# Transposes moved from TensorE to the DMA crossbar, with a reordered first stage, in an attention and feed-forward kernel

## The chip, the cores and the metric

The kernel runs on one core of one Trainium2 chip. The metric is device time in microseconds (us): the median of several executions. The span of a profile is a little shorter than the time of its execution (456.9 us of 459.06 us before). TensorE is called PE in the profile, its weight loads PEld, VectorE DVE, ScalarE ACT, GpSimd POOL, SyncE SP; POOLq and SPq are the queues on which the last two issue transfers.

## The reference

```python
# q, k, v: 8 batches x 8 heads x 576 positions x 64; 8 global positions
scores = q @ k.T / sqrt(64)
mask = (abs(pos_i - pos_j) <= 32) | is_global[i] | is_global[j]
attn = softmax(where(mask, scores, -1e9))
x = (attn @ v), heads side by side: 4608 tokens x 512
out = x + sigmoid(x @ w_res) * ((gelu(x @ w_gate) * (x @ w_val)) @ w_out)   # d_ff = 1536
```

Inputs and output are f32; the kernel multiplies in bf16.

## The kernel before

A first stage prepares batch 0 and does the attention of the first 512 tokens. Then nine chunks of 512 tokens follow. Twelve steps of the feed-forward input (`ffn_in`) run while the next batch is prepared; sixteen slots of the feed-forward output follow, interleaved with the attention of the next chunk. Instructions keep the order in which the program emits them on each engine. These are the parts that the argument touches (cuts are marked with `# ...`):

```python
def zero_qk(i):                       # fills: unused half of qz, edge columns of kt
    for u in range(2):
        zero_wide(qz[i], 64 - 64 * u, 64, u * S, [[2 * S, NP], [1, S]])
    zero_wide(kt[i], 0, 128, 0, [[S + 64, NP], [1, 32]])           # columns 0..31
    zero_wide(kt[i], 0, 128, 32 + S, [[S + 64, NP], [1, 32]])      # columns 608..639

def zero_rest(i):
    nc.vector.memset(ve[i][:, :, :, D:VG], 1.0)                    # the ones column of ve
    # ... edge partitions of ve, parts of gt and ptg

def prep_pair(b, p, what):            # queries or keys of two heads, batches 1 to 7
    src = q_st if what == "q" else k_st
    ps = pss.tile([128, S], BF16, name=f"t{what}", tag="sc")
    for r in range(NQT):              # 5 tiles of positions
        n = min(128, S - 128 * r)
        nc.tensor.transpose(ps[:, 128 * r:128 * r + n], src[0:n, r, 128 * p:128 * p + 128], ident[0:n, 0:n])
    if what == "q":
        nc.scalar.copy(qt[b % 2][:, p, :], ps)
    else:
        nc.vector.tensor_copy(kt[b % 2][:, p, 32:32 + S], ps)

def turn_x(c, t):                     # attention output of 128 tokens -> xt, the input of ffn_in
    # ... PSUM tile tx
    for kk in range(NKT):             # 4
        nc.tensor.transpose(tx[:, kk, :], xtok[c % 2][:, t, 128 * kk:128 * kk + 128], ident)
    (nc.scalar.copy if c == 0 else nc.vector.tensor_copy)(xt[c % 2][:, :, 128 * t:128 * t + 128], tx)

# end of the first stage: loads that cast to bf16, all on GpSimd's queue
load_qk(1)
load_gate_cols(1024, 1536)            # last third of w_gate and w_val
load_v(1)
# ... w_res, w_out in two halves, gathers of the global rows

for c in range(NCH):
    b = c + 1
    # ... load_v(b) for b > 1
    for j in range(NFF):              # 12 steps
        ffn_in(c, j)
        if c == 0:                    # fills of the second set of buffers
            if j == 0: zero_qk(1)
            elif j == 1: zero_rest(1); hot_rows(1)
            # ...
            if j >= 4: prep_pair(b, (j - 4) // 2, "qk"[j % 2])
        elif j < 8: prep_pair(b, j // 2, "qk"[j % 2])
        # ... c == 1 and j == 8: spread_qk, global rows of the later batches
        if j == (11 if c == 0 else 8):
            shift_v(b); load_qk(b + 1); prep_qz(b, 0, NP)
    # ... slots: scores at 0..7, then for t in 0..3
    #     slots[5 + 2 * t].append(values(c + 1, t))
    #     slots[7 + 2 * t].insert(0, turn_x(c + 1, t))
    # ... each slot runs its list and then a quarter of ffn_out; ffn_out ends with
    #     GpSimd's add into ob and nc.sync.dma_start(out[...], ob)
```

`qt`, `qz`, `kt`, `ve`, `vo`, `gt` and `ptg` exist twice, for even and odd batches.

The softmax here doesn't subtract the row's maximum and nothing guards it: scores larger than these inputs give would overflow.

Of the kernel before, what the change touches and what calls it, by code (L numbers as in the profile page):

```python
# [23 lines left out]
def kernel(  # L24
# [23 lines left out]
    CH = 8  # L48
# [67 lines left out]
    nc.scalar.dma_start(gpi, bass.AP(tensor=g32.tensor, offset=g32.offset, ap=[[0, 16], [2, NG], [1, 1]]))  # L116
    for p in range(NP):
        for src, what in ((q, "q"), (k, "k")):
# [9 lines left out]
    nc.gpsimd.memset(ident, 0.0)  # L128
    nc.gpsimd.affine_select(out=ident, in_=ident, pattern=[[-1, 128]], channel_multiplier=1, base=0,
                            compare_op=ALU.not_equal, fill=1.0)  # L130

    blk = const.tile([128, 16], BF16, name="blk", tag="blk")
    nc.gpsimd.memset(blk, 1.0)
    nc.gpsimd.affine_select(out=blk, in_=blk, pattern=[[-8, 16]], channel_multiplier=1, base=0,
                            compare_op=ALU.is_ge, fill=0.0)
    nc.gpsimd.affine_select(out=blk, in_=blk, pattern=[[8, 16]], channel_multiplier=-1, base=7,
                            compare_op=ALU.is_ge, fill=0.0)
# [20 lines left out]
    def zero_rest(i):  # L158
        nc.vector.memset(ve[i][:, :, :, D:VG], 1.0)
        zero(ve[i][0:32, 0, :, :])  # L160
        zero(ve[i][96:128, 4, :, :])
        zero_wide(gt[i], 0, 128, 0, [[1, 64]])
        zero_wide(gt[i], 0, 128, 64 + S, [[1, 64]])
        zero_wide(ptg[i], 0, 128, 64 * (i % 2), [[128, 5], [1, 64]])
# [4 lines left out]

    sel = const.tile([128, 128], BF16, name="sel", tag="sel")  # L170
# [6 lines left out]
    hrow = const.tile([128, 1], I32, name="hrow", tag="hrow")  # L177
    nc.vector.tensor_single_scalar(hrow, ip, 3, ALU.logical_shift_right)
# [11 lines left out]
    gather("q", 0)  # L190
    load_v(0)
    gather("v", 0)
    load_gate_cols(0, 512)
    load_gate_cols(512, 1024)
# [8 lines left out]
    for n in range(1, B // 2):  # L203
        nc.vector.tensor_single_scalar(idx[:, n:n + 1], idx[:, 0:1], float(2 * H * S * n), ALU.add)
    far = const.tile([128, S], F32, name="far", tag="far")
    nc.scalar.activation(far, iota_f, ACTF.Square, bias=ngp, scale=1.0)
    band = const.tile([128, 64], BF16, name="band", tag="band")
# [5 lines left out]
    nc.gpsimd.memset(band, 1.0)  # L213
    nc.gpsimd.affine_select(out=band, in_=band, pattern=[[-1, 64]], channel_multiplier=1, base=0,
                            compare_op=ALU.is_ge, fill=0.0)
    nc.gpsimd.affine_select(out=band, in_=band, pattern=[[1, 64]], channel_multiplier=-1, base=64,
                            compare_op=ALU.is_ge, fill=0.0)

    def masks():
# [9 lines left out]
        nc.vector.scalar_tensor_tensor(maskg, far, 1024.5, nong, ALU.is_gt, ALU.mult)  # L229

    def hot_rows(i):
        r0 = 64 - 64 * (i % 2)
        nc.vector.tensor_copy(gt[i][r0:r0 + 64, 64:64 + S], hot[r0:r0 + 64, :])
# [6 lines left out]
    def spread_qk(n0, n1):  # L240
        nn = n1 - n0
        for what, big, pstep in (("k", kgz, 144), ("q", qgz, 16)):
# [6 lines left out]
            for e in range(2):  # L249
                shift = 64 * e if what == "k" else 0  # L250
                for u in range(2):
                    nc.vector.tensor_copy(
                        view(big, 64 * u, 64, (2 * n0 + e) * width + shift + 8 * u,
                             [[2 * width, nn], [pstep, NP], [1, NG]]),
                        view(tg, 64 * u, 64, 64 * e + 8 * u, [[128, nn], [16, NP], [1, NG]]))
# [41 lines left out]
    def prep_pair(b, p, what):  # L297
        src = q_st if what == "q" else k_st
        ps = pss.tile([128, S], BF16, name=f"t{what}", tag="sc")
        for r in range(NQT):  # L300
            n = min(128, S - 128 * r)
            nc.tensor.transpose(ps[:, 128 * r:128 * r + n], src[0:n, r, 128 * p:128 * p + 128], ident[0:n, 0:n])  # L302
        if what == "q":
            nc.scalar.copy(qt[b % 2][:, p, :], ps)  # L304
        else:
            nc.vector.tensor_copy(kt[b % 2][:, p, 32:32 + S], ps)
# [264 lines left out]
```

## Time and profile before

| | before |
|---|---|
| time, median of 3 | 461.24 us (460.74 to 461.93) |
| span of the profile; TensorE busy | 456.9 us; 91% |
| global scores of batch 0 start | 32.30 us |
| first feed-forward matmul (first `g_ps`) | 46.3 us |
| `g_ps` of chunk 1, of chunk 2 | 94.65, 144.62 us |
| chunks 2 to 6, mean | 46.47 us each |

A chunk is measured here from its first `g_ps` to that of the next.

```profile
DMA  9999999999999999999999999991010000999999
```

### The profile page before, as it was taken

The numbers are of one execution on the slowest core, as the hardware profiler recorded it, in microseconds if no ns is written. First come the engines' busy times: TensorE is split into PE (matmuls) and PEld (weight loads), VectorE is DVE, ScalarE is ACT, GpSimd is POOL, SyncE is SP. The second block draws the span as 40 slices with busy tenths as digits, with TensorE's granted clock in tenths as the row PEclk, the third lists the DMA queues.
The fourth block names the chain that finished last, engine by engine and source line by source line (L and its number), as shares of the span: only waits on it lengthen the run. The fifth ranks groups of instructions, "written<-read, shape, count | busy, mean of one in ns | idle before, by whom it ended". The sixth has DMA issues, their size and how long they took to land.

```text
span 456.9 us, 7784 instructions
## 1 busy us (share of the span) xinstructions
PE 415.2 (91%) x3119; PEld 232.2 (51%) x3170; DVE 234.7 (51%) x465; ACT 182.6 (40%) x291; POOL 166.6 (36%) x187
## 2 busy tenths in 40 slices
PE   2038899999799999999999999999999999999995
PEld 2027445644465556545654465546554664465442
DVE  6277655634774456435554555355535554364421
ACT  4105445243343345334524462436243623543321
POOL 6965618150594271327133712471240121022013
PEclk9999999999999999999999999999999999999999
DMA  7999939283093990199119921994190010001001
GB/s 192 157 193 185 197 80 96 57 91 54 2 99 97 100 103 24 47 123 101 29 47 122 90 39 47 121 79 50 47 103 20 24 44 28 0 25 70 0 23 70
DMA packets 117092, 35.18 MB, mean 77 GB/s; under 512 B 104576, under 2 KB 111232, under 8 KB 117056
## 3 DMA queue, kind: packets, MB, share of 16 engines
q0 software_dynamic: 108784, 18.62, 54.4%
q1 hardware_dynamic: 8128, 16.06, 11.3%
q8 instruction: 25, 0.41, 0.4%
q14 instruction: 11, 0.09, 0.1%
q10 hardware_dynamic: 144, 0.00, 0.0%
HBM read 39.19 MB, written 9.44 MB: 106 GB/s over the span
## 4 chain that ended last, share of the span: by engine, by line
PE 87%; DVE 5%; POOL 3%; issue 2%; DMA 1%; ACT 1%; POOLq 0%; DVEq 0%
PE g_ps L405 22%; PE v_ps L409 20%; PE f_ps L432 20%; PE r_ps L422 7%; PE nd L377 3%; PE sc L351 3%; PE tk L302 2%; PE tq L302 2%; PE nd L371 2%; PE sn L339 2%; PE sg L317 2%; PE tx L397 2%; DVE qz L310 1%; DMA gpi<-in_global_idx_dram 1%; POOL ve L98 1%
## 5 line engine op out<-in xcount | busy, mean ns | idle before, releaser
L413 DVE SCALAR_TENSOR_TENSOR ht<-gsb,v_ps 128x512 bf16<-128x512 bf16 x108 | 73.9, 687 | 111.8 <-PE v_ps L409 85.1
L438 POOL TENSOR_TENSOR ob<-prb,xtok 128x512 f32<-128x512 f32 x36 | 41.8, 1160 | 203.6 <-DVE prb L436 203.5
L412 ACT ACTIVATE gsb<-g_ps 128x512 bf16<-128x512 f32 x108 | 64.5, 597 | 120.6 <-PE g_ps L405 111.5
L405 PE MATMUL g_ps<-xt,wg_t 128*128 128x512 bf16 x431 | 111.4, 380 | 1.4 <-ACT xt L398 0.7
L409 PE MATMUL v_ps<-xt,wv_t 128*128 128x512 bf16 x415 | 108.8, 379 | 0.5
L432 PE MATMUL f_ps<-wo_t,ht 128*128 128x512 bf16 x408 | 101.8, 379 | 1.3
L409 PEld LDWEIGHTS <-wv_t 128*128 128x128 bf16 x432 | 42.3, 98 | 51.0 <-issue 0.2
L405 PEld LDWEIGHTS <-wg_t 128*128 128x128 bf16 x432 | 37.8, 98 | 41.1 <-issue 1.4
L432 PEld LDWEIGHTS <-ht 128*128 128x128 bf16 x432 | 38.5, 98 | 34.0
L354 ACT ACTIVATE pt<-sc 128x512 bf16<-128x512 f32 x72 | 41.9, 597 | 30.6 <-PE sc L351 30.5
L425 ACT ACTIVATE rsb<-r_ps 128x512 bf16<-128x512 f32 x36 | 21.5, 596 | 65.6 <-PE r_ps L422 51.4
L90 POOL DMA_DIRECT2D q_st<-in_q_dram x35 | 30.4, 890 | 41.6 <-PE tq L302 41.4
L356 DVE TENSOR_TENSOR pt<-pt,maskw 128x512 bf16<-128x512 bf16 x72 | 31.0, 435 | 25.8 <-ACT pt L354 24.5
L436 DVE SCALAR_TENSOR_TENSOR prb<-rsb,f_ps 128x512 f32<-128x512 bf16 x36 | 24.6, 684 | 29.4 <-PE f_ps L432 29.2
L422 PE MATMUL r_ps<-wr_t,xt 128*128 128x512 bf16 x135 | 36.3, 379 | 0.4
L98 POOL DMA_DIRECT2D ve<-in_v_dram x40 | 33.9, 867 | 1.8 <-DMA k_st<-in_k_dram 1.8
L90 POOL DMA_DIRECT2D k_st<-in_k_dram x35 | 31.1, 910 | 4.6 <-DMA wg_t<-in_moe_w_gate_dram 1.6
L351 PE MATMUL sc<-qz,kt 128*128 128x128 bf16 x288 | 27.9, 224 | 1.0 <-DVE qz L310 0.9
L351 PEld LDWEIGHTS <-kt 128*128 128x128 bf16 x288 | 21.4, 100 | 11.2 <-issue 1.0
L304 ACT COPY qt<-tq 128x576 bf16<-128x576 bf16 x28 | 17.9, 638 | 16.8 <-PE tq L302 16.8
L391 DVE TENSOR_TENSOR xtok<-nd,rden 128x512 bf16<-128x512 f32 x34 | 23.5, 691 | 1.2
L377 PEld LDWEIGHTS <-pt 128*128 128x128 bf16 x576 | 22.3, 97 | 1.0
(103 smaller groups left out, 371.2 us busy)
## 6 DMA issues: line engine op xcount, KB each, us to landing
out_dram<-ob SPq DMA_DIRECT2D x36, 256.0 KB, 2.0
vo<-ve SPq DMA_DIRECT2D x16, 260.0 KB, 3.7
q_st<-in_q_dram POOLq DMA_DIRECT2D x28, 128.0 KB, 4.2
k_st<-in_k_dram POOLq DMA_DIRECT2D x28, 128.0 KB, 4.7
ve<-in_v_dram POOLq DMA_DIRECT2D x24, 128.0 KB, 4.4
ve<-in_v_dram POOLq DMA_DIRECT2D x16, 96.0 KB, 7.9
wg_t<-in_moe_w_gate_dram POOLq DMA_DIRECT2D x3, 512.0 KB, 6.4
wv_t<-in_moe_w_val_dram POOLq DMA_DIRECT2D x3, 512.0 KB
```

The source lines that it names most:

```text
L90: nc.gpsimd.dma_start(dst[0:n, r, :].rearrange("p (h d) -> p h d", d=D), src[b].rearrange("h s d -> s h d")[128 * r:128 * r + n])
L98: nc.gpsimd.dma_start(t[p0:p1, c, :, 0:D], v[b].rearrange("h s d -> s h d")[s0 + p0:s0 + p1])
L351: nc.tensor.matmul(sc[:, n, :, :], kt[b % 2][:, p, 64 * i:64 * i + 128], qz[b % 2][:, p, :, 64 * i:64 * i + 64], start=True, stop=True)
L354: nc.scalar.activation(mine, sc, ACTF.Exp, bias=0.0, scale=SCALE)
L377: nc.tensor.matmul(nds[h // 4][:, VG * (h % 4):VG * (h % 4) + VG], view(pt, 0, 128, c0, [[1, 128]]), vw, start=False, stop=(h % 4 == 3 and ...
L405: nc.tensor.matmul(g_ps, wg_t[:, kk, 128 * j:128 * j + 128], x[:, kk, :], start=(kk == 0), stop=(kk == NKT - 1))
L409: nc.tensor.matmul(v_ps, wv_t[:, kk, 128 * j:128 * j + 128], x[:, kk, :], start=(kk == 0), stop=(kk == NKT - 1))
L412: nc.scalar.activation(gsb, g_ps, ACTF.Gelu, bias=0.0, scale=1.0)
L413: nc.vector.scalar_tensor_tensor(ht[:, j, :], gsb, 0.5, v_ps, ALU.mult, ALU.mult)
L422: nc.tensor.matmul(r_ps, xt[c % 2][:, kk, 128 * t:128 * t + 128], wr_t[:, kk, :], start=(kk == 0), stop=(kk == NKT - 1))
L432: nc.tensor.matmul(held["f"], ht[:, j, 128 * t:128 * t + 128], wo_t[:, j, :], start=(j == 0), stop=(j == NFF - 1))
L438: nc.gpsimd.tensor_tensor(ob, prb, xtok[c % 2][:, t, :], ALU.add)
```

## The change

The intent is to take transposes off the bounding engine: the queries and keys of batches 1 to 7, and the inputs of chunks 1 to 8, are transposed by the DMA crossbar, from SyncE's queue. The first stage's fills and masks are spread over the engines so that TensorE starts sooner.

```diff
-    def prep_pair(b, p, what):
-        # ... five TensorE transposes and a copy
+    def turn_qk(b):
+        for src, dst, c0 in ((q_st, qt[b % 2], 0), (k_st, kt[b % 2], 32)):
+            for r in range(NQT):
+                n = min(128, S - 128 * r)
+                nc.sync.dma_start(dst[:, :, c0 + 128 * r:c0 + 128 * r + n], src[0:n, r, :], transpose=True)
...
     def turn_x(c, t):
+        mine = xt[c % 2][:, :, 128 * t:128 * t + 128]
+        if c:
+            nc.sync.dma_start(mine, xtok[c % 2][:, t, :], transpose=True)
+            return
...
     for c in range(NCH):
         b = c + 1
         if b < B:
+            turn_qk(b)
             if b > 1:
                 load_v(b)
...
                     elif j == 1:
-                        zero_rest(1)
+                        zero_rest(1, nc.vector)
-                    if j >= 4:
-                        prep_pair(b, (j - 4) // 2, "qk"[j % 2])
-                elif j < 8:
-                    prep_pair(b, j // 2, "qk"[j % 2])
+                if c == 1:
+                    if j == 6:            # was 8
+                        spread_qk(1, B // 2)
...
-                if j == (11 if c == 0 else 8):
+                if j == 8:
                     shift_v(b)
# first stage, in words: the band mask made ahead of GpSimd's transfer issues; fill of pt to ScalarE;
# zero_rest(0) to GpSimd; load of the global positions on SyncE; masks before the first transposes;
# hot_rows and the qgz copies to ScalarE; w_gate and w_val columns 512:1024 loaded later
```

More of the change, by code (lines that the diff above doesn't have):

```diff
@@ L115 @@
     g32 = global_idx.bitcast(I32)
-    nc.scalar.dma_start(gpi, bass.AP(tensor=g32.tensor, offset=g32.offset, ap=[[0, 16], [2, NG], [1, 1]]))
+    nc.sync.dma_start(gpi, bass.AP(tensor=g32.tensor, offset=g32.offset, ap=[[0, 16], [2, NG], [1, 1]]))
     for p in range(NP):
@@ L127 @@
     ident = const.tile([128, 128], BF16, name="ident", tag="ident")
+    band = const.tile([128, 64], BF16, name="band", tag="band")
+    blk = const.tile([128, 16], BF16, name="blk", tag="blk")
     nc.gpsimd.memset(ident, 0.0)
-    nc.gpsimd.affine_select(out=ident, in_=ident, pattern=[[-1, 128]], channel_multiplier=1, base=0,
-                            compare_op=ALU.not_equal, fill=1.0)
-    blk = const.tile([128, 16], BF16, name="blk", tag="blk")
+    nc.gpsimd.memset(band, 1.0)
     nc.gpsimd.memset(blk, 1.0)
-    nc.gpsimd.affine_select(out=blk, in_=blk, pattern=[[-8, 16]], channel_multiplier=1, base=0,
-                            compare_op=ALU.is_ge, fill=0.0)
-    nc.gpsimd.affine_select(out=blk, in_=blk, pattern=[[8, 16]], channel_multiplier=-1, base=7,
-                            compare_op=ALU.is_ge, fill=0.0)
+    for t, pattern, mult, base, op, fill in (
+            (ident, [[-1, 128]], 1, 0, ALU.not_equal, 1.0),
+            (band, [[-1, 64]], 1, 0, ALU.is_ge, 0.0), (band, [[1, 64]], -1, 64, ALU.is_ge, 0.0),
+            (blk, [[-8, 16]], 1, 0, ALU.is_ge, 0.0), (blk, [[8, 16]], -1, 7, ALU.is_ge, 0.0)):
+        nc.gpsimd.affine_select(out=t, in_=t, pattern=pattern, channel_multiplier=mult, base=base,
+                                compare_op=op, fill=fill)
     def zero(ap):
@@ L156, in zero_qk, with zero_rest @@
         zero_wide(kt[i], 0, 128, 32 + S, [[S + 64, NP], [1, 32]])
-    def zero_rest(i):
-        nc.vector.memset(ve[i][:, :, :, D:VG], 1.0)
-        zero(ve[i][0:32, 0, :, :])
-        zero(ve[i][96:128, 4, :, :])
-        zero_wide(gt[i], 0, 128, 0, [[1, 64]])
-        zero_wide(gt[i], 0, 128, 64 + S, [[1, 64]])
-        zero_wide(ptg[i], 0, 128, 64 * (i % 2), [[128, 5], [1, 64]])
+    def zero_rest(i, eng):
+        eng.memset(ve[i][:, :, :, D:VG], 1.0)
+        eng.memset(ve[i][0:32, 0, :, :], 0.0)
+        eng.memset(ve[i][96:128, 4, :, :], 0.0)
+        eng.memset(gt[i][:, 0:64], 0.0)
+        eng.memset(gt[i][:, 64 + S:128 + S], 0.0)
+        eng.memset(ptg[i][:, :, 64 * (i % 2):64 * (i % 2) + 64], 0.0)
     def zero_globals(b0, b1):
@@ L168, in zero_globals @@
         zero_wide(qgz, 0, 128, b0 * NP * 16, [[1, (b1 - b0) * NP * 16]])
+    hrow = const.tile([128, 1], I32, name="hrow", tag="hrow")
+    nc.vector.tensor_single_scalar(hrow, ip, 3, ALU.logical_shift_right)
+    none = const.tile([128, 1], F32, name="none", tag="none")
+    zero(none)
+    nc.scalar.copy(view(pt.bitcast(F32), 0, 128, 32, [[64, H * CH], [1, 32]]),
+                   view(none, 0, 128, 0, [[0, H * CH], [0, 32]]))
     sel = const.tile([128, 128], BF16, name="sel", tag="sel")
@@ L174 @@
     zero_globals(0, 2)
-    hrow = const.tile([128, 1], I32, name="hrow", tag="hrow")
-    nc.vector.tensor_single_scalar(hrow, ip, 3, ALU.logical_shift_right)
     idx = const.tile([128, B // 2], I32, name="idx", tag="idx")
@@ L190 @@
     gather("q", 0)
+    zero_rest(0, nc.gpsimd)
     load_v(0)
@@ L193 @@
     load_gate_cols(0, 512)
-    load_gate_cols(512, 1024)
     gpc = const.tile([128, 1], F32, name="gpc", tag="gpc")
@@ L205 @@
     far = const.tile([128, S], F32, name="far", tag="far")
-    nc.scalar.activation(far, iota_f, ACTF.Square, bias=ngp, scale=1.0)
-    band = const.tile([128, 64], BF16, name="band", tag="band")
     diag = const.tile([128, H], BF16, name="diag", tag="diag")
@@ L212 @@
     maskw = const.tile([128, NWM, 64], BF16, name="maskw", tag="maskw")
-    nc.gpsimd.memset(band, 1.0)
-    nc.gpsimd.affine_select(out=band, in_=band, pattern=[[-1, 64]], channel_multiplier=1, base=0,
-                            compare_op=ALU.is_ge, fill=0.0)
-    nc.gpsimd.affine_select(out=band, in_=band, pattern=[[1, 64]], channel_multiplier=-1, base=64,
-                            compare_op=ALU.is_ge, fill=0.0)
     def masks():
@@ L228, in masks @@
                                     view(band, 0, 128, 0, [[0, n], [1, 64]]), ALU.mult)
-        nc.vector.scalar_tensor_tensor(maskg, far, 1024.5, nong, ALU.is_gt, ALU.mult)
     def hot_rows(i):
         r0 = 64 - 64 * (i % 2)
-        nc.vector.tensor_copy(gt[i][r0:r0 + 64, 64:64 + S], hot[r0:r0 + 64, :])
+        nc.scalar.copy(gt[i][r0:r0 + 64, 64:64 + S], hot[r0:r0 + 64, :])
     twice = {what: const.tile([128, B // 2, 2, D], BF16, name=f"{what}gd", tag=f"{what}gd") for what in "kq"}
@@ L251, in spread_qk @@
                 for u in range(2):
-                    nc.vector.tensor_copy(
+                    (nc.scalar.copy if what == "q" else nc.vector.tensor_copy)(
                         view(big, 64 * u, 64, (2 * n0 + e) * width + shift + 8 * u,
@@ L294, in turn_pair @@
                                   ps.rearrange("c r s -> c s r"))
-    def prep_pair(b, p, what):
-        src = q_st if what == "q" else k_st
-        ps = pss.tile([128, S], BF16, name=f"t{what}", tag="sc")
-        for r in range(NQT):
-            n = min(128, S - 128 * r)
-            nc.tensor.transpose(ps[:, 128 * r:128 * r + n], src[0:n, r, 128 * p:128 * p + 128], ident[0:n, 0:n])
-        if what == "q":
-            nc.scalar.copy(qt[b % 2][:, p, :], ps)
-        else:
-            nc.vector.tensor_copy(kt[b % 2][:, p, 32:32 + S], ps)
+    def turn_qk(b):
[3 more added lines that the diff above has]
+                nc.sync.dma_start(dst[:, :, c0 + 128 * r:c0 + 128 * r + n], src[0:n, r, :], transpose=True)
     def prep_qz(b, p0, p1):
@@ L394, in turn_x @@
     def turn_x(c, t):
-        tx = bank([128, NKT, 128], "tx", BF16) if c == 0 else pss.tile([128, NKT, 128], BF16, name="tx", tag="sc")
+        mine = xt[c % 2][:, :, 128 * t:128 * t + 128]
+        if c:
+            nc.sync.dma_start(mine, xtok[c % 2][:, t, :], transpose=True)
+            return
+        tx = bank([128, NKT, 128], "tx", BF16)
         for kk in range(NKT):
             nc.tensor.transpose(tx[:, kk, :], xtok[c % 2][:, t, 128 * kk:128 * kk + 128], ident)
-        (nc.scalar.copy if c == 0 else nc.vector.tensor_copy)(xt[c % 2][:, :, 128 * t:128 * t + 128], tx)
+        nc.scalar.copy(mine, tx)
     def ffn_in(c, j):
@@ L443, in ffn_out @@
         return [gate, third(0), third(1), third(2)]
-    zero_wide(pt, 0, 128, 64, [[128, H * CH], [1, 64]])
     cast = {}
@@ L451 @@
                 cast[what] = cast_pair(p, what), cast.get(what, (None,))[0]
+        if p == 0:
+            masks()
         if p == 1:
-            masks()
-            hot_rows(0)
+            nc.scalar.activation(far, iota_f, ACTF.Square, bias=ngp, scale=1.0)
         if p:
@@ L458 @@
             prep_qz(0, p - 1, p)
-    zero_rest(0)
+    hot_rows(0)
     spread_qk(0, 1)
+    nc.vector.scalar_tensor_tensor(maskg, far, 1024.5, nong, ALU.is_gt, ALU.mult)
     shift_v(0)
@@ L465 @@
     spread_v(0, 1)
-    spread_vg(0, nc.vector)
+    spread_vg(0, nc.gpsimd)
+    load_gate_cols(512, 1024)
     for p in range(1, NP):
@@ L509 @@
                         spread_vg(1, nc.vector)
-                    if j >= 4:
-                        prep_pair(b, (j - 4) // 2, "qk"[j % 2])
-                elif j < 8:
-                    prep_pair(b, j // 2, "qk"[j % 2])
-                if c == 1 and j == 8:
-                    spread_qk(1, B // 2)
-                    spread_v(1, B // 2)
-                    for n in range(2, B):
-                        spread_vg(n, nc.gpsimd)
-                if j == (11 if c == 0 else 8):
+                if c == 1:
+                    if j == 6:
+                        spread_qk(1, B // 2)
+                        spread_v(1, B // 2)
+                    elif j == 8:
+                        for n in range(2, B):
+                            spread_vg(n, nc.gpsimd)
+                if j == 8:
                     shift_v(b)
```

## The prediction

> **What bounds the kernel now.** I read the page first: busy shares and the chain that ended last. TensorE (PE) is busy for 91% of the span, no other engine for more than 51%, and the chain, followed back from the last instruction, lies on TensorE for 87%.
>
> ```profile
> span 456.9 us, 7784 instructions
> PE 415.2 (91%) x3119; PEld 232.2 (51%) x3170; DVE 234.7 (51%) x465; ACT 182.6 (40%) x291; POOL 166.6 (36%) x187
> PE 87%; DVE 5%; POOL 3%; issue 2%; DMA 1%; ACT 1%; POOLq 0%; DVEq 0%
> ```
>
> So what TensorE no longer does is saved, unless what replaces it arrives late. The clock row is 9 in all 40 slices, so throttling is no part of this. Next I read the timeline of a middle chunk. First its feed-forward part, TensorE alone (columns: start, duration, line, tiles, count; durations of pipelined groups overlap, so I go by starts):
>
> ```profile
> 292.36 0.52 PE L302 MATMUL tk<-ident,k_st 128*128 128x128 bf16 x5
> 292.81 1.04 PE L405 MATMUL g_ps<-xt,wg_t 128*128 128x512 bf16 x4
> 293.69 1.03 PE L409 MATMUL v_ps<-xt,wv_t 128*128 128x512 bf16 x4
> 294.55 0.52 PE L302 MATMUL tq<-ident,q_st 128*128 128x128 bf16 x5
> 295.00 1.04 PE L405 MATMUL g_ps<-xt,wg_t 128*128 128x512 bf16 x4
> ...
> 303.30 1.03 PE L405 MATMUL g_ps<-xt,wg_t 128*128 128x512 bf16 x4
> 304.17 1.03 PE L409 MATMUL v_ps<-xt,wv_t 128*128 128x512 bf16 x4
> 305.03 1.03 PE L405 MATMUL g_ps<-xt,wg_t 128*128 128x512 bf16 x4
> ```
>
> The reader should see the pace: a step with five transposes takes 295.00 - 292.81 = 2.19 us, one without takes 305.03 - 303.30 = 1.73 us. A step's transposes cost TensorE 0.46 us, fully on the path.
>
> Then the end of the chunk before it, all engines:
>
> ```profile
> 279.97 0.69 DVE L391 TENSOR_TENSOR xtok<-nd,rden 128x512 bf16<-128x512 f32 x1
> 280.18 0.74 PEld L422 LDWEIGHTS <-xt 128*128 128x128 bf16 x4
> 280.39 1.03 PE L422 MATMUL r_ps<-wr_t,xt 128*128 128x512 bf16 x4
> 280.69 0.69 DVE L436 SCALAR_TENSOR_TENSOR prb<-rsb,f_ps 128x512 f32<-128x512 bf16 x1
> 281.04 0.42 PEld L397 LDWEIGHTS <-xtok 128*128 128x128 bf16 x4
> 281.26 0.39 PE L397 MATMUL tx<-ident,xtok 128*128 128x128 bf16 x4
> 281.43 2.31 PEld L432 LDWEIGHTS <-ht 128*128 128x128 bf16 x12
> 281.46 1.16 POOL L438 TENSOR_TENSOR ob<-prb,xtok 128x512 f32<-128x512 f32 x1 [4.25 <-DVE prb L436]
> ```
>
> The last input tile xtok is complete at 280.66, its transposes take 281.43 - 281.04 = 0.39 us of weight loading, and the next chunk's first matmul (g_ps) starts at 284.07.
>
> The first stage is another matter: TensorE idles there. This is its timeline:
>
> ```profile
> 19.17 0.24 POOL L216 TENSOR_SCALAR_AFFINE_SELECT band<-band 128x64 bf16<-128x64 bf16 x1
> 19.44 0.63 DVE L227 TENSOR_TENSOR maskw<-nong,band 128x576 bf16<-128x576 bf16 x2 [8.96 <-POOL band L216]
> ...
> 23.76 0.66 PE L289 MATMUL tk<-ident,k_st 96*128 96x96 bf16 x6 [11.90 <-DVE k_st L283]
> ```
>
> VectorE (DVE) stood for 8.96 us before its mask product, because the small band mask is made on GpSimd (POOL) behind 8.6 us of DMA issues; behind VectorE, TensorE stood 11.90 us.
>
> **What the Trainium skill says.** (1) "VectorE: DVE Perf Modes", The three transpose paths: a 128x128 bf16 transpose takes 390 ns on TensorE and 1309 ns on the DMA crossbar, the latter landing in SBUF. The trace disagrees with the first for back-to-back use: 0.46 us for five is 0.09 us each. No crossbar transpose is in the trace before. (2) "DMA: Bandwidth & Descriptors", Latency and other measured facts: DMA transposes reached 261 GB/s in one kernel; by it 128 KB need 0.5 us. (3) "Advanced Engine Details and Errata", DMA Advanced Topics: transposing DMAs on trn2 are as fast as regular ones, though its table calls hardware descriptor generation the worse of the two for transposes. Nothing in this trace decides between these.
>
> **The change part by part.**
>
> 1. Queries and keys of batches 1 to 7: 7 x 8 = 56 groups of five TensorE transposes go, 56 x 0.46 = **25.8 us**, all on the path. The PSUM copies go with them (28 x 0.638 us on ScalarE, 28 x 0.451 us on VectorE), which are off the path and count for nothing.
>
> 2. Inputs of chunks 1 to 8: 32 groups of four transposes go, 32 x 0.39 = **12.5 us**. Their 32 VectorE copies of 0.425 us are mostly hidden.
>
> 3. Added: 102 crossbar transposes on SyncE's queue, in order with the other DMAs there. Ten per batch start at the chunk's beginning, needed by VectorE's query copy in step 8, 8 x 1.73 = 13.8 us later. By (1) and (2) a 128x512 transpose needs about 1.3 + 0.4 us to land; issue is my guess, 0.45 us as for the DMAs on that queue now, up to 1 us. Ten, overlapped, take 5 to 10 us; they start some 2.5 us late, behind the last output store. So they fit, with 1 to 6 us to spare: **0**.
>
> 4. The last input transpose of a chunk has no such room. In the issue order it stands behind the output store of tile 2, which waits for GpSimd's add ending 281.46 + 1.16 = 282.62. Store issue 0.45, transpose issue 0.45, landing 1.7: 285.2. TensorE, without tx, would be ready at 284.07 - 0.39 = 283.7. That is a new wait of 1.5 us, and 2.5 us with an issue of 1 us and a little more latency. I take 2.1 us, on 8 chunks: **+17 us**. In this part of the chunk the transfers have the DMA engines nearly alone (columns: window, span, busy of PE, PEld, DVE, ACT, POOL, clock, DMA, GB/s):
>
> ```profile
> 312.00:314.00 2.00, 2.00 (x17) 1.15 (x16) 0.90 (x3) 1.51 (x4) 0.00 (x0) 1.00 0.00 0
> 318.00:320.00 2.00, 2.00 (x21) 1.30 (x19) 1.76 (x5) 0.60 (x1) 0.00 (x0) 1.00 0.04 15
> ```
>
> 5. First stage. The band mask moves ahead of GpSimd's DMA issues, the 1.76 us fill of pt to ScalarE, the fills of ve, gt and ptg (28.73 to 30.46) to GpSimd. Re-adding VectorE's rows from 8.3 us in the new order, with the last key tile landing near 14 us, I get the global scores at about 21 us instead of 32.3: 11 us. Against it: GpSimd's fills delay the first value loads by about 2.5 us, the shifted values then land near 28 us, just when wanted, and the weights still come at the DMA engines' pace (near 190 GB/s in the first five slices). I keep **8.5 us**.
>
> 6. Chunks 0 and 1: the query copy and the spreading of global rows (half now on ScalarE) move from steps 11 and 8 to 8 and 6. Chunk 1 took 128.68 - 78.50 = 50.2 us between its global rows and the previous ones, later chunks 46.4, so about 3.8 us is lost there and 0.9 us in chunk 0. I expect **2.5 us** back.
>
> Sum: 461.2 - 25.8 - 12.5 - 8.5 - 2.5 + 17 = **429 us**.
>
> **The rivals.** (a) *The transposes are hidden anyway.* If issue is cheap and landing takes 1 us, part 4's wait vanishes: 412 us. The idle DMA engines speak for it; the store in front on the queue speaks against it. (b) *Crossbar or issue is much slower.* If four 128x128 blocks cost four times 1309 ns and do not overlap, one transpose takes 5.2 us, a batch's ten (nine full ones) 47 us against 13.8 us of room; every chunk would wait some 30 us and the kernel would exceed 600 us. At 2 us each it is 18 + 2.5 us, a wait of about 6 us in seven chunks: 429 + 42 = 471 us. Against it: 261 GB/s in (2). For it: the doubtful table entry in (3), and the value loads that share the DMA engines at each chunk's start. (c) *The first stage becomes bound by loads.* Then part 5 gives 3 to 5 us instead of 8.5, or a wait shows in chunk 0 instead: 433 us. (d) *The new waits cost clock.* "TensorE: Matmul & The Clock Gate", Why this matters for your kernels, warns of TensorE gaps over about 3 us; at my 2.1 us nothing follows, at 4 us each chunk would lose more than the gap: about 450 us. No wait of the steady chunks here is that long, so the trace does not test it.
>
> **Range and chances.** (a) and a better first stage set the lower end, 413; (c), or waits of 4 us per chunk, the upper, 447. The removed 38 us are the firmest numbers; the transpose's duration is the softest. Only (b) brings less than 2% gain: 8% for within 2%, 5% for slower, 87% for faster.
>
> **What would show it.** Right: TensorE's step stays at 1.73 us through all 12 steps; a wait of about 2 us before each chunk's first g_ps, ended by the DMA of xt; batch transposes landed before step 8; global scores starting at 20 to 23 us; chunks of about 43.5 us. Wrong: SyncE's transpose issues over 1 us each or landings over 4 us; VectorE's query copy waiting for qt; GpSimd's loads waiting for the transposes to release the staging tiles; the first g_ps later than 41 us.

## More of the kernel before

```profile
52.40 0.09 DVE L159 MEMSET ve<- 128x40 bf16 x1
```

In the transfer summary of the stretch from 20 to 80 us (the busy tenths of the DMA engines in forty slices of 1.5 us) the DMA engines are busy in every slice until 60.5 us, that is for the first 14.2 us of chunk 0, which starts at 46.3 us. Still no wait of TensorE in this run ends with a transfer. In VectorE's timeline (start, duration, line, operation) the fill of the ones column of the second `ve` runs at 52.40 us, without a wait: the value loads of batch 1 were issued from 34.4 to 39.6 us, and the one landing on record took 11.4 us, so they had just come in. The kernel before reaches its loads late enough not to wait for them, though they are still running in chunk 0.

## The result, and the profile after

| | before | after |
|---|---|---|
| time, median of 4 each, same chip | 461.41 us (460.74 to 461.93) | 449.61 us (448.51 to 450.32) |
| ratio of times | 1 | 0.9743 (95%: 0.9715 to 0.977) |
| global scores; first `g_ps` | 32.30; 46.3 us | 20.07; 34.3 us |
| `g_ps` of chunk 1, of chunk 2 | 94.65, 144.62 us | 98.98, 147.55 us |
| chunks 2 to 6, mean | 46.47 us | 43.66 us |
| chunk 7; tail | 40.05; 39.89 us | 40.96; 40.01 us |

A ratio is the mean time of one kernel's fast runs over that of the other's of the same rounds, so it is not quite the ratio of the medians quoted. The kernel became faster by 2.6%, but 449.61 us lies above the range of 413 to 447 us, and 20.6 us above the predicted time.

The page after, at its head (span and instructions; busy time, share and instructions by engine; then the granted clock in tenths over forty slices of 11 us, and the shares of the chain that ended last):

```profile
span 446.8 us, 7136 instructions
...
PE 387.6 (87%) x2718; PEld 207.3 (46%) x2762; DVE 204.5 (46%) x388; ACT 169.5 (38%) x274; POOL 167.2 (37%) x194
...
PEclk9999569999899999999999999999999999999999
...
PE 54%; issue 21%; DMA 13%; POOL 5%; DVE 3%; ACT 1%; SPq 1%; POOLq 0%; DVEq 0%
```

TensorE's busy time fell by 27.6 us but the span by only 10.1 us. TensorE's share fell from 91% to 87%, and the clock row, 9 throughout before, has a 5 and a 6 in the fifth and sixth slice, that is from 45 to 67 us. The chain now runs through transfers for 13%. So TensorE waits for something, early.

The landmarks say where. The feed-forward part starts 12.0 us sooner (the texts below say 12.4 us; the trace has the first `g_ps` at 34.30 us). At the end of chunk 0 the kernel is 4.33 us behind the one before, so chunk 0 took 16.4 us longer. Chunk 1 gives back 1.4 us and chunks 2 to 6 give 14.1 us; chunk 7 and the tail cost 1.0 us. Together, 12.0 - 16.4 + 1.4 + 14.1 - 1.0 = 10.1 us.

The list of waits after (engine, line, what it waited for: us in total, times, longest):

```profile
DVE kt L149 <- DMA kt<-k_st: 19.5, 1, 19.5
PE v_ps L406 <- DVE ht L410: 19.3, 2, 17.7
...
PE g_ps L402 <- DMA xt<-xtok: 12.9, 8, 1.7
```

Eight of the waits are the predicted ones, before each chunk's first `g_ps`: 12.9 us, 1.6 us each. The 19.5 us and the 17.7 us are single events, and the prediction has nothing like them. The timelines of SyncE's queue, VectorE and TensorE show what they are (start, duration, engine, line, operation; in brackets idle time before it and what ended it):

```profile
35.30 7.69 SPq L299 DMA_TRANSPOSE qt<-q_st  x5
43.09 10.35 SPq L299 DMA_TRANSPOSE kt<-k_st  x5
```

```profile
38.56 1.02 DVE L149 MEMSET qz<- 64x1152 f32 x1 [0.28 <-issue]
59.08 0.19 DVE L149 MEMSET kt<- 128x64 f32 x2 [19.51 <-DMA kt<-k_st]
59.19 0.67 DVE L410 SCALAR_TENSOR_TENSOR ht<-gsb,v_ps 128x512 bf16<-128x512 bf16 x1
```

```profile
41.20 1.03 PE L402 MATMUL g_ps<-xt,wg_t 128*128 128x512 bf16 x4
59.91 1.86 PE L406 MATMUL v_ps<-xt,wv_t 128*128 128x512 bf16 x4 [17.68 <-DVE ht L410]
61.57 1.72 PE L402 MATMUL g_ps<-xt,wg_t 128*128 128x512 bf16 x4
```

VectorE comes to the fill of the edge columns of the second `kt` at step 0 of chunk 0. The crossbar transposes of batch 1's keys into the same tile were emitted before it. They write columns 32 to 607, the fill writes 0 to 31 and 608 to 639, and still the fill waits until the last of them has landed, at 59.08 us. VectorE's products of the feed-forward steps stand behind the fill in its order, the PSUM tiles that they read are not released, and TensorE stands for 17.68 us. Afterwards a group of four matmuls takes 61.57 - 59.91 = 1.66 us instead of 0.86 us, the half clock of the page.

In a steady chunk nothing of this kind is left. SyncE's queue and VectorE there (chunk 4 starts at 234.78 us):

```profile
231.89 0.34 SPq L437 DMA_DIRECT2D out_dram<-ob  x1
232.33 1.22 SPq L390 DMA_TRANSPOSE xt<-xtok  x1
...
235.77 6.65 SPq L299 DMA_TRANSPOSE qt<-q_st  x5
242.51 6.48 SPq L299 DMA_TRANSPOSE kt<-k_st  x5
```

```profile
251.20 1.79 DVE L303 COPY qz<-qt 64x2304 bf16<-64x2304 bf16 x2
```

The issue of a crossbar transpose takes 1.2 to 1.3 us, against 0.34 us of the store before it. Ten of them end at 248.99 us, and VectorE's copy from `qt` at 251.20 us has no wait in brackets. The last input transpose is issued at 232.33 us, right after the output store.

### The profile page after: what moved, and what is told of

Same layout as the page of the kernel before. It is cut to its first block, busy times and chain, and to the rows that moved or that the text cites. A ratio compares the mean times of both kernels' runs of the same rounds, so it can differ in the third digit from the quotient of the medians.

```text
span 446.8 us, 7136 instructions
## 1 busy us (share of the span) xinstructions
PE 387.6 (87%) x2718; PEld 207.3 (46%) x2762; DVE 204.5 (46%) x388; ACT 169.5 (38%) x274; POOL 167.2 (37%) x194
## 4 chain that ended last, share of the span: by engine, by line
PE 54%; issue 21%; DMA 13%; POOL 5%; DVE 3%; ACT 1%; SPq 1%; POOLq 0%; DVEq 0%
PE g_ps L402 15%; PE v_ps L406 14%; PE f_ps L429 11%; DMA wo_t<-in_moe_w_out_dram 4%; PE r_ps L419 4%; POOL ob L435 3%; DMA xt<-xtok 3%; DMA qt<-q_st 3%; PE sc L344 2%; PE nd L370 2%; DMA wo_t<-in_k_dram 2%; PE sg L310 2%; PE sn L332 1%; PE nd L364 1%; POOL k_st L90 1%
## 5 line engine op out<-in xcount | busy, mean ns | idle before, releaser
L406 PE MATMUL v_ps<-xt,wv_t 128*128 128x512 bf16 x417 | 110.3, 383 | 19.7 <-DVE ht L410 19.3
L402 PE MATMUL g_ps<-xt,wg_t 128*128 128x512 bf16 x429 | 112.1, 383 | 14.0 <-DMA xt<-xtok 12.9
L402 PEld LDWEIGHTS <-wg_t 128*128 128x128 bf16 x432 | 42.0, 99 | 67.2 <-issue 13.3
L90 POOL DMA_DIRECT2D q_st<-in_q_dram x35 | 30.0, 874 | 23.4 <-DMA qt<-q_st 23.4
L98 POOL DMA_DIRECT2D ve<-in_v_dram x40 | 34.3, 870 | 1.5 <-DMA k_st<-in_k_dram 1.5
L370 PE MATMUL nd<-ve,pt 128*128 128x65 bf16 x320 | 22.3, 193 | 0.0
```

The lines of the kernel that those rows point to most:

```text
L90: nc.gpsimd.dma_start(dst[0:n, r, :].rearrange("p (h d) -> p h d", d=D), src[b].rearrange("h s d -> s h d")[128 * r:128 * r + n])
L98: nc.gpsimd.dma_start(t[p0:p1, c, :, 0:D], v[b].rearrange("h s d -> s h d")[s0 + p0:s0 + p1])
L370: nc.tensor.matmul(nds[h // 4][:, VG * (h % 4):VG * (h % 4) + VG], view(pt, 0, 128, c0, [[1, 128]]), vw, start=False, stop=(h % 4 == 3 and ...
L402: nc.tensor.matmul(g_ps, wg_t[:, kk, 128 * j:128 * j + 128], x[:, kk, :], start=(kk == 0), stop=(kk == NKT - 1))
L406: nc.tensor.matmul(v_ps, wv_t[:, kk, 128 * j:128 * j + 128], x[:, kk, :], start=(kk == 0), stop=(kk == NKT - 1))
```

## The experiments

After the result I had a theory for chunk 0 and two rivals. The theory: the fills behind the transfers cost the time. The rivals: the supply of loads bounds chunk 0 whatever the fills do; or the time is lost elsewhere in the new order. The other terms of the sum had to be tested as well. Each text names its theories by its own letters. All ten runs gave correct results. The ratios are against runs of the kernel before on the same chip, whose medians were 460.04 us (e1 to e4), 460.32 us (e5 to e8) and 459.82 us (e9, e10). In the table, "fills early" means that the fills of the second set of `kt` edges, `ve`, `gt` and `ptg` are done in the first stage.

| run | batch 1 | batches 2 to 7 | inputs | first stage | fills early | g_ps of chunk 1 | time | ratio |
|---|---|---|---|---|---|---|---|---|
| before | TensorE | TensorE | TensorE | old | no | 94.65 | 461.24 | 1 |
| after | crossbar | crossbar | crossbar | new | no | 98.98 | 449.61 | 0.9743 |
| e1 | crossbar | crossbar | crossbar | new | kt only | 100.37 | 451.15 | 0.9805 |
| e2 | crossbar | crossbar | crossbar, early | new | no | 98.88 | 436.11 | 0.9462 |
| e3 | crossbar | crossbar | TensorE | new | no | 100.02 | 443.62 | 0.9630 |
| e4 | TensorE | TensorE | TensorE | new | no | 95.19 | 462.21 | 1.0044 |
| e5 | crossbar | crossbar | crossbar | new | yes | 96.50 | 447.25 | 0.9716 |
| e6 | TensorE | crossbar | crossbar | new | yes | 85.47 | 439.20 | 0.9536 |
| e7 | crossbar | crossbar | crossbar, early | new | yes | 94.33 | 432.36 | 0.9402 |
| e8 | crossbar | crossbar | crossbar | old | no | 103.59 | 452.76 | 0.9838 |
| e9 | TensorE | crossbar | crossbar, early | new | yes | 84.80 | 424.00 | 0.9219 |
| e10 | TensorE | TensorE | TensorE | new | yes | 83.64 | 448.73 | 0.9764 |

### e1: the fill of kt's edges ahead of the transposes

```diff
     def zero_qk(i):
         # ... the fill of qz
+        if i == 0:
+            zero_pads(i)
+
+    def zero_pads(i):
         # ... the two fills of kt's edges
@@ end of the first stage
+    zero_pads(1)
     shift_v(0)
```

> The fills of the second key tile's edges are made on VectorE in the first stage, before any crossbar transpose writes that tile; nothing else changes. Theory A (the fill that stands behind the key transposes costs the whole stall): VectorE's 19.5 us wait and TensorE's 17.7 + 1.6 us wait in chunk 0 vanish and nothing takes their place, 449.6 - 19.3 = about 430 us. Theory B (the stall hides a shortage of transfers: in the changed kernel the two halves of w_out landed only at about 68 and 71.6 us, and would now be wanted from about 57 us on): the fill's wait vanishes, but TensorE waits some 8 to 11 us in chunk 0 for keys or for w_out, 438 to 442 us. Theory C (the fill was not the cause): about 449 us.

Measured: 451.15 us (450.93 to 452.34), 0.9805 (0.9768 to 0.9842). The gain failed to come. The list of waits of this run:

```profile
DVE ve L165 <- DMA ve<-in_v_dram: 22.2, 1, 22.2
PE v_ps L410 <- DVE ht L414: 20.7, 1, 20.7
```

The wait on `kt` is gone, and the next fill, of the ones column of `ve` at step 1, waits 22.2 us for the value loads of batch 1. Those lie in the same tile and were emitted earlier too. The theory in its first form, that this one fill costs the time, fell; a second wait stood right behind the first. The time is that of theory C, but the run doesn't show C, that the fill was no cause: the next wait hides what the first was worth.

### e2: input transposes earlier on SyncE's queue

```diff
-                slots[7 + 2 * t].insert(0, lambda t=t: turn_x(c + 1, t))
+                slots[5 + 2 * t].append(lambda t=t: turn_x(c + 1, t))
```

> Each crossbar transpose of an input tile is issued straight after its tile is made, two slots earlier, so the last one stands ahead of the output store of tile 2 on SyncE's queue instead of behind it. Theory A (the eight waits of about 1.6 us before each chunk's first g_ps come from standing behind that store): they vanish, 12.9 us, 436 to 438 us. Theory B (the wait is the transposes' own duration or their queue): the waits stay above 1 us, 446 us or more.

Measured: 436.11 us (434.39 to 436.38), 0.9462 (0.9424 to 0.9501). The waits of `g_ps` for `xt` are gone from the list, and chunks 2 to 6 take 41.88 us each instead of 43.66 us. Each transpose now stands ahead of an output store that waits for GpSimd's add, and not behind it. TensorE's timeline of this run at the same boundary:

```profile
226.99 2.75 PE L429 MATMUL f_ps<-wo_t,ht 128*128 128x512 bf16 x12
229.58 1.03 PE L402 MATMUL g_ps<-xt,wg_t 128*128 128x512 bf16 x4
```

The next chunk starts 229.58 - 226.99 = 2.59 us after the start of the last output group, which is the pace of twelve matmuls. The wait of chunk 0 is unchanged (18.7 us), so the two are separate. The wait of part 4 was a matter of order on the queue.

### e3: inputs on TensorE again

The edit puts back the `turn_x` of the kernel before; nothing else differs from the changed kernel.

> The inputs of all chunks are transposed on TensorE again; queries and keys stay on the crossbar. Theory A (that part of the change paid back what it took: 32 groups of 0.39 us removed, 12.5 us, against 12.9 us of new waits for the last tile): 448 to 451 us, the same as the changed kernel, with no wait of g_ps on a transfer. Theory B (the waits would exist without it too): 461 us.

Measured: 443.62 us (442.84 to 444.76), 0.9630 (0.9596 to 0.9665). I had not expected this: taking the inputs off the crossbar again makes the changed kernel 5 to 6 us faster (6.0 us by the medians, 5.2 us by the ratios, the two having run on different chips). TensorE's timeline of this run:

```profile
223.60 0.39 PE L390 MATMUL tx<-ident,xtok 128*128 128x128 bf16 x4
223.83 0.39 PE L344 MATMUL sc<-qz,kt 128*128 128x128 bf16 x4
```

By its starts a group of four transposes costs TensorE 223.83 - 223.60 = 0.23 us; the 0.39 us are the length of a pipelined group, of which the next group covers a part. The chunks agree: 42.78 us here against 41.88 us in e2 is 0.90 us, about 4 x 0.23. So 32 groups are worth 7.4 us, less than the 12.9 us that the new waits cost.

### e4: the new first stage alone

The edit puts back both TensorE transposes and the chunk order of before; only the first stage is the new one.

> The first stage as changed, but queries, keys and inputs all transposed on TensorE as before, no crossbar at all. Theory A (the first stage is worth what its own timeline shows, first g_ps at about 34 us instead of 46.3): 461.4 - 12.4 = 449 us, so the whole measured gain of the change. Theory B (an earlier first stage runs ahead of the weight loads and waits for them in chunk 0): 452 to 457 us, with TensorE waiting for w_gate, w_val or w_out.

Measured: 462.21 us (461.83 to 462.74), 1.0044 (1.0008 to 1.0079): no gain at all, though the feed-forward part starts about 12 us sooner. My text did not have the size. The list of waits of this run:

```profile
DVE ve L161 <- DMA ve<-in_v_dram: 12.8, 1, 12.8
...
PE v_ps L413 <- DVE ht L417: 10.9, 1, 10.9
```

The same fill of `ve`, which ran at 52.40 us without a wait before, is reached sooner now and waits for the value loads. The start is earlier; the loads are not.

### e5: all fills early

```diff
     load_gate_cols(0, 512)
+    zero_rest(1, nc.gpsimd)
...
+    zero_pads(1)
     shift_v(0)
...
                     elif j == 1:
-                        zero_rest(1, nc.vector)
                         hot_rows(1)
```

> All of VectorE's fills of the second buffers that stood behind transfers into the same tiles go ahead of those transfers: the key tile's edges on VectorE, the value tile's ones and zeros (and the fills of gt and ptg) on GpSimd, both in the first stage; the crossbar transposes stay. Theory A (fills behind transfers are the whole of the stall; the run before moved only one of two): no wait takes their place, 428 to 431 us. Theory B (the transfers themselves come too late for an earlier start, w_out landing at about 68 and 72 us): chunk 0 now waits for batch 1's keys and queries or for w_out, some 8 to 11 us instead of 21, 437 to 442 us.

Measured: 447.25 us (446.42 to 447.5), 0.9716 (0.9683 to 0.9749), a smaller gain than I had expected. Both fills' waits are gone. TensorE's waits in this run are on the weights themselves; one of them, from its timeline:

```profile
70.60 1.89 PE L434 MATMUL f_ps<-wo_t,ht 128*128 128x512 bf16 x4 [3.67 <-DMA wo_t<-in_moe_w_out_dram]
```

Such waits also stand before `w_val` (2.0 us), `w_gate` (1.8 us) and `w_res` (1.6 us), with the 4.4 us for `w_out` 9.8 us in all, and half clock follows. These are the waits of theory B, in its size of 8 to 11 us; its time of 437 to 442 us was missed all the same. A third layer thus lies under the two fills: the weights come too late for the earlier start.

### e6: e5, and batch 1 transposed on TensorE

```diff
         if b < B:
-            turn_qk(b)
             if b > 1:
+                turn_qk(b)
                 load_v(b)
...
+                    if j >= 4:                # in chunk 0
+                        prep_pair(b, (j - 4) // 2, "qk"[j % 2])
...
-                if j == 8:
+                if j == (11 if c == 0 else 8):
```

> As the run with all fills early, but batch 1 alone is transposed on TensorE, so that its ten crossbar transposes don't share the DMA engines with the weights. Theory A (no shortage): 3.7 us slower than the run with all fills early. Theory B (shortage of transfers in the first 70 us): w_out lands some 7 us earlier, as in the run with the first stage alone, TensorE waits 0 to 3 us for it, 431 to 435 us, so faster than the run with all fills early.

Measured: 439.2 us (437.7 to 439.99), 0.9536 (0.9498 to 0.9575). Eight groups more on TensorE (8 x 0.46 = 3.7 us) make the kernel 8 us faster than e5, and chunk 0 ends 11.0 us sooner. The windows from 50 to 60 us of e5 and of e6, in this order (length; busy time and count of PE, PEld, DVE, ACT, POOL; granted clock; share of the DMA engines, which passes 1 where packets overlap; GB/s):

```profile
50.00:60.00 10.00, 7.24 (x25) 2.77 (x26) 2.80 (x4) 1.79 (x3) 2.97 (x4) 0.83 1.77 129
```

```profile
50.00:60.00 10.00, 9.92 (x63) 5.12 (x62) 3.49 (x6) 3.28 (x7) 5.84 (x7) 1.00 1.60 208
```

With the crossbar transposes among the loads the DMA engines are as busy but move 129 GB/s; without them 208 GB/s, and TensorE is busy for 9.92 us of the 10 at full clock. Not all of the 129 and 208 compares like with like, since the runs are at different loads by then. The transfer summary by queue from 40 to 60 us does (packets, MB, share of the time of 16 engines; q0 carries GpSimd's loads, q1 SyncE's transfers), e5 and then e6:

```profile
q0 software_dynamic: 7847, 1.90, 105.0%
q1 hardware_dynamic: 4856, 1.17, 58.1%
```

```profile
q0 software_dynamic: 9613, 3.35, 164.5%
q1 hardware_dynamic: 160, 0.53, 9.2%
```

From 30 to 40 us both runs loaded 1.73 MB on q0. In the next 20 us the loads themselves fell back by 3.35 - 1.90 = 1.45 MB while 1.17 MB of transposes went beside them. In e5 GpSimd's issues wait longer for earlier loads (4.0 us for `k_st`, against 0.9 us in e6). There the first half of `w_out` was issued at 50.97 us and landed 19.6 us later, and TensorE waited for it; in e6 it was issued at 46.17 us, and TensorE starts on it at 64.15 us without a wait.

The run missed its 431 to 435 us by some 4 us. The late input transposes are still in it, and the first of these waits is the longest (TensorE's timeline):

```profile
85.47 1.71 PE L418 MATMUL g_ps<-xt,wg_t 128*128 128x512 bf16 x4 [2.46 <-DMA xt<-xtok]
```

The group after it runs at half clock, 86.97 - 85.47 = 1.50 us later instead of 0.86, and chunk 1 takes 51.1 us.

### e7: e5, with the input transposes early

The edit is that of e2, made in e5.

> All fills early and each input tile's crossbar transpose issued straight after the tile is made. The two gains lie in different parts of a chunk and should add: 13 us less than the run with all fills early (424 to 429 us by theory B, 415 to 418 us by theory A). If they don't add, SyncE's queue or the DMA engines tie them together.

Measured: 432.36 us (430.69 to 435.0), 0.9402 (0.9349 to 0.9455), 14.9 us below e5. Between the changed kernel and e2 the same edit brought about 13 us. The two causes add up. The 424 to 429 us were missed because they start from e5's expected time and not from its measured 447.25 us. One wait of 3.1 us for `xt` stays, before chunk 1.

### e8: crossbar transposes and the new chunk order, old first stage

The edit puts back the first stage of before and leaves the rest as changed, except that `hot_rows` and the copies into `qgz` are back on VectorE in chunks 0 and 1 too.

> The crossbar transposes and the order of the chunks as changed, with the first stage as before. Theory A (chunk 0 starts when the transfers allow, so the earlier first stage is worth nothing): VectorE's fill of the key tile waits for batch 1's key transposes here too, but some 10 us instead of 20, and the time is that of the changed kernel, 446 to 453 us. Theory B (the first stage's 12.4 us are real and add to the rest): 460 us or more.

Measured: 452.76 us (452.22 to 453.47), 0.9838 (0.9805 to 0.9871). Both fills wait here too, 8.1 us for the keys and 3.3 us for the values, less than in the changed kernel, which fits a first stage that reaches them later. The new first stage adds 1% to this (0.9743 against 0.9838), about 4 us of the 12 us by which it starts sooner.

### e9: e6, with the input transposes early

The edit is that of e2, made in e6.

> All three remedies: fills ahead of the transfers, batch 1 transposed on TensorE, each input tile's crossbar transpose issued straight after the tile. Theory A (they lie in different places and add): the run with fills early and batch 1 on TensorE, 439.2 us, less 13 us: 424 to 428 us, the fastest of all. Theory B (any earlier chunk 0 runs into the transfers again): about 432 us, as with the fills early and the inputs early.

Measured: 424.0 us (423.84 to 424.83), 0.9219 (0.9203 to 0.9234), as expected, and the fastest of all. Its page:

```profile
span 423.0 us, 7196 instructions
...
PE 389.7 (92%) x2757; PEld 209.6 (50%) x2802; DVE 205.5 (49%) x386; ACT 172.2 (41%) x278; POOL 169.2 (40%) x200
```

TensorE does about the same work as in the changed kernel (389.7 us against 387.6 us), in a span shorter by 23.8 us. So the gain is waits and half clock removed, and not work.

### e10: new first stage and early fills, all transposes on TensorE

The edit is that of e5, made in e4.

> The first stage as changed and all fills ahead of the transfers, but no crossbar at all. Without crossbar transposes w_out landed at about 61 and 64 us in the run with the first stage alone, and TensorE would want it from about 61 us on. Theory A (the first stage is worth something once no fill waits and nothing shares the DMA engines with the weights): 8 to 10 us under the kernel before, 451 to 454 us. Theory B (the first stage is worth nothing in any case): 458 to 462 us.

Measured: 448.73 us (447.54 to 449.59), 0.9764 (0.9748 to 0.978), a little better than expected. Against e4 the early fills bring about 13 us, 11.6 us of it by the end of chunk 0. The first stage's gain was there all along and stood behind one fill.

## Why the prediction was wrong

The direction was right; the time was 20.6 us too low. I put the prediction's parts into landmarks and compared. Chunk 1 should have begun at 94.65 - 8.5 (part 5) - 8 x 0.46 (part 1) - 0.9 (part 6) + 2.1 - 4 x 0.39 (parts 4 and 2) = 82.1 us; it began at 98.98 us, **16.9 us** later. In the same way chunk 1 is 3.3 us too long, chunks 2 to 6 together 1.6 us, chunk 7 and the tail 0.5 us. This is the whole miss of the span, 446.8 us against 456.9 - 32.3 = 424.6 us; the miss of the time is smaller, chiefly because the profiled execution of before was 2.2 us faster than the 461.24 us from which the sum starts. That the steady chunks came so close, 0.3 us each, is partly luck: part 2 counts 0.64 us a chunk too much of gain, part 4 some 0.3 us or more too much of wait.

1. **Queries and keys, 25.8 us: right.** Chunks 2 to 6 with TensorE's inputs take 42.78 us in e3 against 46.47 us before: 3.69 us, 8 x 0.46.

2. **Inputs, 12.5 us: mis-sized.** I took the length of the weight loads of four transposes, 0.39 us, for their cost. By the starts, the way I had read part 1, it is 0.23 us: 7.4 us in all (e2, e3).

3. **"So they fit, with 1 to 6 us to spare: 0": this step failed.** In steady chunks it holds: ten transposes are issued in 13.2 us, the copy does not wait. It holds in spite of an issue of 1.2 to 1.3 us where I had guessed 0.45 us, up to 1. In chunk 0 it does not. I had asked only when the transposes are needed, by the copy in step 8. I did not ask what else touches their destination: the fill of `kt`'s edges, emitted after them and wanted at step 0. It waited 19.5 us. My own list of what would show the step wrong names slow issues and landings, VectorE's copy and GpSimd's loads, not a fill. Three of these signs came: issues over 1 us, landings over 4 us (a median of 7.1 us for `qt`, 5.2 us for `kt`), and the loads, which wait 23.4 us in 12 waits of `q_st`. But no later chunk loses time by them: with inputs early chunks 2 to 6 take 41.88 us (e2), which is 46.47 - 3.69 - 4 x 0.23 us. The second thing that I did not ask is what the ten transposes do to the loads beside them: in chunk 0 the loads themselves came later (e5 against e6), and with the fills early chunk 0 ends 11.0 us later for it, although TensorE then has 3.7 us less to do.

4. **The new wait: right in kind, a little too large.** I had 2.1 us a chunk; the list of waits has 1.6 us, and the chunks of e2 against those of the change 43.66 - 41.88 = 1.8 us. e2 removed it by order alone, which shows that the store ahead of it on the queue was the cause. Parts 2 and 4 together make the crossbar for the inputs a loss of 12.9 - 7.4 = 5.5 us in this order; e3 measured 5 to 6 us. Rival (a), the hidden transfer, came true with e2's order and not with this one (its 412 us lay below the range's own lower end of 413). Rival (d) did not show in these waits: the groups behind them run at full clock.

5. **First stage, 8.5 us: the start right, the worth wrong.** The global scores started at 20.07 us where I had 21, and the first `g_ps` came 12.0 us sooner. Alone it was worth nothing (e4), on top of the crossbar about 1% (e8 against the change), with the fills early about 11 us (e10). Rival (c), "a wait shows in chunk 0 instead", was this case, and I had sized it at 4 us.

6. **2.5 us back in chunks 0 and 1: it did not come.** Chunk 1 is now 4.9 us longer than a steady one, where it was 3.5 us. The timeline of TensorE after shows two waits close together where the global rows are spread at step 6, and half clock behind them:

```profile
112.54 0.34 PE L245 MATMUL tg<-ident,kgd 128*128 128x128 bf16 x3 [1.53 <-DVE kgd L241]
114.42 0.50 PE L245 MATMUL tg<-ident,qgd 128*128 128x128 bf16 x3 [1.54 <-DVE qgd L241]
114.72 1.91 PE L402 MATMUL g_ps<-xt,wg_t 128*128 128x512 bf16 x4
116.42 1.60 PE L406 MATMUL v_ps<-xt,wv_t 128*128 128x512 bf16 x4
```

   The first group takes 116.42 - 114.72 = 1.70 us instead of 0.86, the next, by the start of the one behind it at 117.86 us, 1.44 us: together 1.4 us more, which is the difference. The waits themselves are not new. The kernel before has them at the same place, at full clock:

```profile
115.37 0.34 PE L247 MATMUL tg<-ident,kgd 128*128 128x128 bf16 x3 [1.32 <-DVE kgd L243]
117.25 0.34 PE L247 MATMUL tg<-ident,qgd 128*128 128x128 bf16 x3 [1.54 <-DVE qgd L243]
```

   Nor does the step decide: in e4, which spreads at step 8 like the kernel before, waits of 1.32 and 1.54 us are followed by half clock, and chunk 1 takes 52.33 us instead of 49.97 us. So no gain from the move to step 6 shows, and half clock took 1.4 us on top. No run moved the spreading alone.

Chunk 0 needs both of its causes to be told. The `g_ps` of chunk 1, with the new first stage (e4 and e10 also have the later batches and the inputs on TensorE, which in chunk 0 touches only the four inputs at its end):

| | fills in place | fills early |
|---|---|---|
| batch 1 by the crossbar | 98.98 us (after) | 96.50 us (e5) |
| batch 1 on TensorE | 95.19 us (e4) | 85.47 us (e6), 83.64 us (e10) |

Either remedy alone brings 2.5 or 3.8 us; together they bring 13.5 to 15.3 us. The fill's wait is what the changed kernel's trace shows, and it hides the other cause: ten crossbar transposes in the stretch where the loads for chunk 0 already keep the DMA engines busy. With both undone chunk 1 begins at 84.80 us in e9, 2.7 us from the 82.1 us of the prediction, which had counted on TensorE losing batch 1's 3.7 us, and the rest of e9 can be had from the sum: 429 - 17 (part 4 gone) + 12.5 - 7.4 (part 2 at its size) + 8 x 0.46 (batch 1 on TensorE) = 420.8 us. It measured 424.0 us, 3.2 us more (4.6 us, if it is allowed for that the kernel before took 459.82 us on that chip and not 461.2 us). The 2.5 us of part 6, which did not come, are most of it; the rest is not explained.

What stays open: beside the transposes the loads moved 1.90 MB where they otherwise moved 3.35 MB, but no run shows by what rule the DMA engines share their time between the two. e6 also moves the shift of `v` and the next loads in chunk 0 from step 8 to step 11; in e5 these transfers start at 62.75 us and later, after the stretch that is compared here. Why half clock follows some waits of 1.5 to 2.5 us and not others was not tested. The two waits at the spreading of the global rows stand in all twelve kernels, and half clock follows them in all but the kernel before and e10, the two in which TensorE has no wait of over 2 us in or right after chunk 0. That is seen together, not shown to be the cause.

## What to carry to other kernels

When a write into a buffer turns into a transfer, look for every other instruction that touches the same tile, also its disjoint edges, and emit the fills ahead of any transfer into it. An engine that waits in order for such a fill stops all that stands behind it, and clearing one wait may only show the next. Before you count an earlier start as gain, add up the bytes that must have come in by the first need. On a queue kept in order, issue a transpose as soon as its source is ready and ahead of a store that waits for someone else, and compare its wait with what it takes off the bounding engine as read from starts, not from durations.

## What the Trainium skill lacked or had wrong

- "DMA: Bandwidth & Descriptors", Latency and other measured facts, gives 261 GB/s for DMA transposes; "Advanced Engine Details and Errata", X-Bar Transpose (TRN2), says that they are "as fast as regular DMAs". Neither section gives the time of an issue on trn2, and that set the pace here (the first page has, for trn3, a comparison with "previous generations" in cycles, which doesn't name trn2): 1.2 to 1.3 us for a 128x512 bf16 transpose between SBUF tiles, against 0.34 us for a 256 KB store. Ten of them, 2 x 576 x 512 x 2 bytes = 1.18 MB, were issued in 13.2 us, 89 GB/s.
- "VectorE: DVE Perf Modes", The three transpose paths, has 390 ns for a 128x128 bf16 transpose on TensorE. Back to back, four cost 0.23 us here and five 0.46 us, so 60 to 90 ns each. On the crossbar four such blocks went in one transfer, with 1.2 us of issue and 2.4 us from issue to landing (median of 32).
- "TensorE: Matmul & The Clock Gate", Why this matters for your kernels, warns of gaps over about 3 us. Here one wait of 2.46 us (e6), and two of 1.53 and 1.54 us within 2 us (chunk 1 after), were followed by groups of matmuls at 1.5 to 1.7 us instead of 0.86; the single waits of 1.6 us before the steady chunks, and the two of 1.32 and 1.54 us in the kernel before, were not. So the length of one gap alone does not tell these cases apart.
- No page that I read says that a fill of columns disjoint from those of a transfer waits for that transfer when both lie in one tile, as the framework ordered it here: 19.5 us (after), 22.2 us (e1), 12.8 us (e4).
- No page that I read says what crossbar transposes cost the loads beside them: 1.90 MB of loads in 20 us with 1.17 MB of transposes (e5), 3.35 MB without (e6).
